# Turning kv with a TensorE transpose and a 16-column product in place of one 144-column product

## The chip, the cores and the metric

The kernel runs on one core of a Trainium2 chip. The metric is device time in microseconds (us), as the median of several executions; one more execution is recorded by the hardware profiler, and all rows below are from it.

## The reference, cut to what matters

Random-feature attention is followed by a mixture of experts with cosine routing. B = 8 batches, H = 8 heads, S = 576 positions, 64 values a head, 128 features; E = 8 experts, and x has 4608 rows of 512.

```python
phi(x) = concat([cos(x @ omega.T), sin(x @ omega.T)], -1) / sqrt(128)
q_p, k_p = phi(q), phi(k)                      # (b, h, s, 256)
kv  = einsum('bhsm,bhsd->bhmd', k_p, v)        # 256 x 64 for each head
z   = sum(k_p, axis=2)
num = einsum('bhsm,bhmd->bhsd', q_p, kv)
den = einsum('bhsm,bhm->bhs', q_p, z)          # kept away from 0
x   = (num / den), heads side by side          # (4608, 512)
logits = normed(x) @ normed(expert_emb).T / tau
e   = argmax(logits); g = softmax(logits)[e]
out = g * (relu(x @ w1[e]) @ w2[e])
```

## The kernel before

The attention runs in 32 steps, `steps[n] = (b, i)`: one batch and a pair of heads (i and i + 4) a step. The order of the work on every engine is written out by hand in the loop `for n in range(1, NS - 1)`, and what stands in it is software-pipelined: one pass of the loop holds work of steps n - 1 to n + 4. On TensorE a pass issues, in this order: `proj_q(n)` (L251), `num(n - 1)` (L373), `proj_k(n + 2)` (L238), `turns(n + 3)` (L213 and L215, TensorE transposes of k), `kv_products(n + 1)` (L324) and `kv_turn(n)` (L341 and L348).

`kv_products` leaves kv turned: the tile `kvT` holds, for each head `a` of the pair, 128 partitions (64 values for the sine half of the features, 64 for the cosine half) by 128 features. VectorE copies it out of PSUM (`kv_copy`, L334). `kv_turn(n)` then makes of it, in the PSUM region `kvnew`, what `num` needs as its moving operand: 128 features by `W` = 73 columns for each head and half. 64 of these are kv, 8 are kv times the head's part of the normed expert embedding (from which the logits are summed later on), and the last one is the sum z (from the tile `zs`, made by GpSimd in `zsum`, by the two columns of `zmask`, L348). The first 72 columns of both halves come out of one float32 product a head: `kvT[:, a]` is the stationary operand (128 x 128), and `rmat[:, i, a]`, of 2 x 72 = 144 columns, the moving one. `rmat` is block-diagonal: an identity of 64 and 8 embedding columns for each half, and zeros. ScalarE copies `kvnew` to the SBUF tile `kv` (`kv_out`, L201).

A float32 product shows as two records in the trace (two weight loads, two passes of the moving operand), a float32 transpose as one of each.

`rmat` is filled during the start-up: GpSimd clears it (L458, L459) and copies the identity into it (`set_up_unit`, L542, eight copies), VectorE adds the embedding columns (`set_up_turn`, L554). GpSimd's queue runs in order: behind `set_up_unit` come `set_up_tables`, `set_up_norms` (L506), `set_up_emb` (L514, which waits for a reciprocal on VectorE, L512, behind L509), `set_up_columns`, a weight transfer, and then the sums `zsum(0, .)` (L309 to L314) over the tile `cok`.

After the attention, 40 blocks of 128 rows go through their experts (L1054, L1087).

Of the kernel before, what the change touches and what calls it, by code (L numbers as in the profile page):

```python
# [11 lines left out]
FP32 = mybir.dt.float32  # L12
# [16 lines left out]
def kernel(  # L29
# [12 lines left out]
    nc = tc.nc  # L42
    B, H, S, Dh = q.shape
    M = omega.shape[0]
    E, D = moe_expert_emb.shape
# [3 lines left out]
    P = 128  # L49
    NPAIR = H // 2  # L50
# [13 lines left out]
    W = 64 + E + 1  # L64
# [7 lines left out]
    persist = ctx.enter_context(tc.tile_pool(name="persist", bufs=1))  # L72

    ident = persist.tile([P, P], FP32)
# [33 lines left out]

    omT2 = persist.tile([P, P], FP32)
    omT4 = persist.tile([P, 2, P], FP32)  # L110
    rmat = persist.tile([P, NPAIR, 2, 2, 64 + E], FP32)
    lsq = persist.tile([P, NSLOT, NG], FP32)
    lmax = persist.tile([P, NSLOT], FP32)
    xin_all = persist.tile([P, XBUF, XW], I32)
# [29 lines left out]
    with tc.tile_pool(name="psA", bufs=1, space=PSUM) as psA, tc.tile_pool(  # L144
# [4 lines left out]
        kvnew = ps[:, 7 * 512 + 2 * W : 7 * 512 + 6 * W].rearrange("p (h a w) -> p h a w", h=2, a=2)  # L149
# [187 lines left out]
        def kv_turn(n):  # L337
            b, i = steps[n]
            d = st[n]
            for a in range(2):  # L340
                nc.tensor.matmul(  # L341
                    kvnew[:, a, :, 0 : W - 1],
                    lhsT=d["kvT"][:, a],
                    rhs=rmat[:, i, a],
                    start=True,
                    stop=True,
                )
                nc.tensor.matmul(  # L348
                    kvnew[:, :, a, W - 1],
                    lhsT=d["zs"][:, a],  # L350
                    rhs=zmask,
                    start=True,
                    stop=True,
                )
# [110 lines left out]
        def set_up_numbers():  # L465
            for par in range(2):
                nc.gpsimd.iota(
                    tok_g[64 * par : 64 * par + 64],
                    pattern=[[2 * S, NGRP], [1, SG]], base=par * S, channel_multiplier=NCH,
                )  # L470
            nc.gpsimd.iota(tmpi[:, 0:P], pattern=[[1, P]], base=0, channel_multiplier=0)

        def set_up_tables():
            nc.gpsimd.memset(tri, 0.0)
            for e in range(1, E):
                nc.gpsimd.memset(tri[:, e, 0:e], 1.0)
            make_identity(nc, ident16)
            make_upper_triangular(nc, sltb, val=1.0, diag=False)
            nc.gpsimd.memset(onesb, 1.0)
# [53 lines left out]
                    rhs=idle.unsqueeze(1).to_broadcast([P, 2, 2 * P]), start=True, stop=True,  # L533
                )

        def set_up_unit():
            for half in range(2):
                r0 = 64 * half
                for a in range(2):
                    d0 = E if a == 0 else 0  # L540
                    for h2 in range(2):
                        nc.gpsimd.tensor_copy(  # L542
                            rmat[r0 : r0 + 64, a::2, h2, half, d0 : d0 + 64],
                            ident[r0 : r0 + 64, r0 : r0 + 64]
                            .unsqueeze(1).to_broadcast([64, NPAIR // 2, 64]),
                        )

        def set_up_turn():
            emb_t = tp_e.rearrange("p (h i e) -> p i h e", h=2, e=E)
            for half in range(2):  # L550
                r0 = 64 * half
                for a in range(2):
                    e0 = 0 if a == 0 else 64
                    nc.vector.tensor_copy(  # L554
                        rmat[r0 : r0 + 64, a::2, :, half, e0 : e0 + E], emb_t[r0 : r0 + 64, a::2]
                    )

        def part(n, which, cols):
# [25 lines left out]
        turns(0)  # L584
        copy_k(0)
        set_up_numbers()
        set_up_unit()
        set_up_tables()
        set_up_norms()
        for b in range(2):  # L590
# [52 lines left out]
        fold(1, "k")  # L643
        kv_copy(0)
        set_up_turn()
        wave(1, "co", "k")
        zsum(1, 1)
# [7 lines left out]
        kv_copy(1)  # L655
        frac(2, "k", slice(0, P))
        kv_turn(0)

        def set_up_routing(n):
# [536 lines left out]
        for n in range(1, NS - 1):  # L1196
# [43 lines left out]
            if k2:  # L1240
                frac(n + 2, "k", slice(0, P))
            kv_turn(n)
            set_up_routing(n)
            route_pe(n)
# [23 lines left out]
        hidden_products(0)  # L1268
        expert_of(1)
        kv_turn(last)  # L1270
        fold(last, "q")
        wave(last, "co", "q")
# [152 lines left out]
```

## Time and profile before

| | |
|---|---|
| median of 3 runs | 453.14 us (452.38 to 454.96) |
| profiled execution, its own time | 451.52 us |
| its span, first to last instruction | 449.7 us |
| mean granted TensorE clock | 0.994 of full speed |
| TensorE busy | 432.5 us (96%) |
| GpSimd busy | 370.0 us (82%) |
| ScalarE busy | 344.0 us (76%) |
| VectorE busy | 327.5 us (73%) |

The span leaves out what lies around the first and the last instruction, 1.8 us here. Busy time of TensorE has modelled ends, so it tells that work followed on work, and not how fast the array was fed; for that the starts of the weight loads (PEld) are read. Times within a row are from the start of the span.

### The profile page before, as it was taken

What the parts mean: (1) busy time and instruction counts of PE and PEld (TensorE: products, weight loads), DVE (VectorE), ACT (ScalarE), POOL (GpSimd) and SP (SyncE); (2) the same over time, 40 slices, a digit from 0 to 9 for tenths busy, and PEclk for the clock granted to TensorE, in tenths of its full rate; (3) what the DMA queues carried; (4) which work ended last, traced back from release to release, by engine and by line L of the source; (5) the groups of instructions that cost most, each with busy time, mean ns of one, the idle gap of its engine ahead of it and who ended that gap; (6) DMA issues with size and microseconds to landing.
All of it is one profiled execution on the core that took longest, in us unless ns stands there. A gap on an engine that the chain in (4) does not pass through costs nothing. (4 is left out here: it accounts for less than half of the span.)

```text
span 449.7 us, 18881 instructions
## 1 busy us (share of the span) xinstructions
PE 432.5 (96%) x7799; PEld 356.4 (79%) x7799; DVE 327.5 (73%) x735; ACT 344.0 (76%) x478; POOL 370.0 (82%) x507
## 2 busy tenths in 40 slices
PE   8999999999999999999999999998999999999992
PEld 4788888989888888889888888876767777777770
DVE  5679977788777789898899989999753554554450
ACT  4878988888888889888888888875556777676741
POOL 8999998988889888889899898987877778777741
PEclk9999999999999999999999999999999999999997
DMA  7999998999999989999898896559577767777530
GB/s 193 200 203 206 205 202 195 194 182 212 200 195 209 197 191 202 188 212 192 176 229 190 177 203 111 102 123 204 149 161 200 183 147 202 164 202 168 151 91 30
DMA packets 80390, 80.32 MB, mean 179 GB/s; under 512 B 32678, under 2 KB 59302, under 8 KB 80304
## 3 DMA queue, kind: packets, MB, share of 16 engines
q1 hardware_dynamic: 59616, 42.59, 40.2%
q0 software_dynamic: 19200, 35.83, 39.3%
q8 instruction: 64, 1.05, 1.0%
q10 hardware_dynamic: 1488, 0.67, 0.7%
q14 instruction: 22, 0.18, 0.1%
HBM read 72.62 MB, written 20.09 MB: 206 GB/s over the span
## 5 line engine op out<-in xcount | busy, mean ns | idle before, releaser
L1054 PEld LDWEIGHTS <-w_sb 128*128 x1280 | 74.6, 98 | 12.5 <-issue 4.3
L373 PE MATMUL ps<-kv,siq 128*64 128x73 f32 x1152 | 76.6, 229 | 0.9 <-DVE gsc L973 0.9
L1087 PE MATMUL ps<-w_sb,coq 128*128 x320 | 75.6, 379 | 0.0
L373 PE MATMUL ps<-kv,coq 128*64 128x73 f32 x1152 | 75.0, 226 | 0.1
L373 PEld LDWEIGHTS ps<-kv,siq 128*64 128x64 f32 x1152 | 58.9, 135 | 12.9 <-issue 10.8
L373 PEld LDWEIGHTS ps<-kv,coq 128*64 128x64 f32 x1152 | 60.1, 137 | 0.2 <-issue 0.2
L278 DVE SCALAR_TENSOR_TENSOR cok<-cok,ps 128x128 f32<-128x128 f32 (+1 forms) x62 | 46.3, 748 | 13.0 <-ACT cok L272 13.0
L1087 PEld LDWEIGHTS <-coq 128*128 128x128 f16 x320 | 29.6, 98 | 28.8 <-DVE coq L1069 0.6
L910 POOL DMA_INDIRECT xin_all<-rf_x,prm x40 | 42.0, 1051 | 11.9 <-issue 8.1
L309 POOL TENSOR_TENSOR zt<-sik 128x384 f32<-128x384 f32 x31 | 39.6, 1277 | 12.8 <-ACT sik L297 12.1
L278 DVE SCALAR_TENSOR_TENSOR coq<-coq,ps 128x1152 f32<-128x1152 f32 x32 | 43.2, 1351 | 5.8 <-ACT coq L272 5.6
L297 ACT ACTIVATE siq<-coq 128x1152 f32<-128x1152 f32 x32 | 37.3, 1164 | 8.3 <-DVE coq L278 7.9
L297 ACT ACTIVATE cok<-cok,pio 128x1152 f32<-128x1152 f32 x31 | 38.9, 1255 | 5.1 <-DVE cok L284 5.0
L251 PE MATMUL ps<-qr,omT 32*128 32x288 f32 x512 | 41.5, 428 | 0.9 <-DVE kvT L334 0.5
L1054 PE MATMUL ps<-qr,w_sb 128*128 128x128 f16 x640 | 39.0, 219 | 3.1 <-DMA qr<-v 2.8
L945 ACT ACTIVATE v<-xin_all 128x512 f16<-128x512 f32 x32 | 20.1, 629 | 27.8 <-issue 15.2
L238 PE MATMUL ps<-omT,kT 64*128 64x128 f32 x522 | 40.7, 284 | 0.6 <-DVE coq L278 0.6
L297 ACT ACTIVATE coq<-coq,pio 128x1152 f32<-128x1152 f32 x32 | 40.2, 1256 | 1.3 <-DVE coq L284 1.2
L314 POOL TENSOR_TENSOR zs<-zs,zt 128x128 f32<-128x128 f32 x64 | 36.2, 566 | 5.0
L1054 PE MATMUL ps<-qx,w_sb 128*128 128x128 f16 x640 | 39.0, 219 | 0.1
L272 ACT ACTIVATE cok<-ps 128x1152 f32<-128x1152 f32 x31 | 35.0, 1129 | 4.6 <-POOL zt L312 1.0
L284 DVE TENSOR_SCALAR cok<-cok 128x1152 int32<-128x1152 int32 x31 | 27.7, 892 | 14.6 <-ACT sik L297 14.1
(214 smaller groups left out, 1171.0 us busy)
## 6 DMA issues: line engine op xcount, KB each, us to landing
w_sb<-in_moe_w_dram POOLq DMA_DIRECT2D x32, 512.0 KB, 8.0
qr<-in_q_dram SPq DMA_DIRECT2D x64, 144.0 KB, 4.9
rf_x<-xb SPq DMA_DIRECT2D x30, 288.0 KB, 4.6
kr<-in_k_dram SPq DMA_DIRECT2D x58, 144.0 KB, 4.7
v<-in_v_dram SPq DMA_DIRECT2D x32, 144.0 KB, 4.6
xin_all<-in_v_dram SPq DMA_DIRECT2D x30, 144.0 KB, 4.9
w_sb<-in_k_dram SPq DMA_DIRECT2D x6, 144.0 KB, 3.1
xin_all<-rf_x,prm POOLq DMA_INDIRECT x40, 3.7
```

Source lines behind the costliest of these rows:

```text
L238: nc.tensor.matmul(kreg[:, KS[c] * P : KS[c] * P + P], lhsT=t[r0 : r0 + 64, j * P : j * P + P], rhs=omT2[r0 : r0 + 64], start=True, stop=True,
L251: nc.tensor.matmul(qreg[:, g // 2, QW * (g % 2) : QW * (g % 2) + QW], lhsT=omT4[r0 : r0 + 32, b], rhs=t[r0 : r0 + 32].rearrange("p (c b j) ...
L272: nc.scalar.activation(dst, src, AF.Copy, bias=CMAGIC, scale=1.0)
L278: nc.vector.scalar_tensor_tensor(out=dst, in0=dst, scalar=CMAGIC, in1=src, op0=ALU.subtract, op1=ALU.subtract)
L284: nc.vector.tensor_scalar(t, t, 0x7FFFFFFF, None, ALU.bitwise_and)
L297: nc.scalar.activation(st[n][which + nm], t, AF.Sin, bias=pio2 if which == "co" else 0.0, scale=-TWO_PI * SINSC,)
L309: nc.gpsimd.tensor_tensor(zt, t[:, 0:3], t[:, 3:6], ALU.add)
L314: nc.gpsimd.tensor_tensor(z, z, zt[:, 2], ALU.add)
L373: nc.tensor.matmul(nm[r0 : r0 + 64, c], lhsT=ph[:, 2 * QW * hh + 64 * c : 2 * QW * hh + 64 * c + 64], rhs=d["kv"][:, hh, half], start=(hal ...
L910: ins = nc.gpsimd.indirect_dma_start(out=t, out_offset=None, in_=x_rows[:], in_offset=bass.IndirectOffsetOnAxis(ap=prm[:, j : j + 1], axis=0),
L1054: nc.tensor.matmul(h_ps[:, f * P : f * P + P], lhsT=weights(k), rhs=d["xT"][:, c * P : c * P + P], start=(c == 0), stop=(c == 3),)
L1087: nc.tensor.matmul(y_ps, lhsT=d["hT"][:, c * P : c * P + P], rhs=weights(NW1 + c), start=(c == 0), stop=(c == NW2 - 1),)
```

## The change

`rmat` keeps only the embedding columns, 2 x 8 for each head. Each head's `kvT` is first turned by a TensorE transpose (stationary `kvT[:, a]`, moving the identity of 128 columns), which writes the 2 x 64 columns of kv, and the product with `rmat`, now of 16 columns, writes the 2 x 8 columns beside them. `set_up_unit` goes.

```diff
-    rmat = persist.tile([P, NPAIR, 2, 2, 64 + E], FP32)
+    rmat = persist.tile([P, NPAIR, 2, 2, E], FP32)
...
         def kv_turn(n):
             b, i = steps[n]
             d = st[n]
+            d0, e0 = (E, 0) if i % 2 == 0 else (0, 64)
+            for a in range(2):
+                nc.tensor.transpose(kvnew[:, a, :, d0 : d0 + 64], d["kvT"][:, a], ident)
             for a in range(2):
                 nc.tensor.matmul(
-                    kvnew[:, a, :, 0 : W - 1],
+                    kvnew[:, a, :, e0 : e0 + E],
                     lhsT=d["kvT"][:, a],
                     rhs=rmat[:, i, a],
...
-        def set_up_unit():
-            for half in range(2):
-                r0 = 64 * half
-                for a in range(2):
-                    d0 = E if a == 0 else 0
-                    for h2 in range(2):
-                        nc.gpsimd.tensor_copy(
-                            rmat[r0 : r0 + 64, a::2, h2, half, d0 : d0 + 64],
...
-                        rmat[r0 : r0 + 64, a::2, :, half, e0 : e0 + E], emb_t[r0 : r0 + 64, a::2]
+                        rmat[r0 : r0 + 64, a::2, :, half], emb_t[r0 : r0 + 64, a::2]
...
-        set_up_unit()
```

On TensorE, at the end of the first pass that holds a `kv_turn` (every later one reads alike; `128x2x72` is the output, and the names behind the arrow are the moving and the stationary operand):

```order
 L324 MATMUL ps<-cok,xin_all 64x128 x2
-L341 MATMUL ps<-rmat,kvT 128x2x72
-L348 MATMUL ps<-zmask,zs 128x2
-L341 MATMUL ps<-rmat,kvT 128x2x72
-L348 MATMUL ps<-zmask,zs 128x2
+L342 MATMUL ps<-ident,kvT 128x2x64 x2
+L344 MATMUL ps<-rmat,kvT 128x2x8
+L351 MATMUL ps<-zmask,zs 128x2
+L344 MATMUL ps<-rmat,kvT 128x2x8
+L351 MATMUL ps<-zmask,zs 128x2
 L251 MATMUL ps<-qr,omT_65 128x288 x8
```

Two transposes (now L342) stand ahead of the four products, whose order is as it was; nothing else in the queue moves.

On GpSimd, in the start-up, before:

```order
L457 MEMSET half_77 128x2
L458 MEMSET rmat 64x8x72
L459 MEMSET rmat 64x8x72
L467 IOTA w_sb 64x36 x2
L471 IOTA w_sb 128x128
L542 COPY rmat<-ident 64x2x64 x8
L474 MEMSET tri 128x64
```

and with the change:

```order
L460 MEMSET half_77 128x2
L461 MEMSET rmat 64x8x8
L462 MEMSET rmat 64x8x8
L470 IOTA w_sb 64x36 x2
L474 IOTA w_sb 128x128
L477 MEMSET tri 128x64
```

The eight copies are gone and the two clearings have a ninth of their columns; what follows keeps its order, so that it stands earlier by that much.

## Rows read from the trace of the kernel before

**Rows 1.** The page, busy time: us (share of the span), instructions.
```profile
PE 432.5 (96%) x7799; PEld 356.4 (79%) x7799; DVE 327.5 (73%) x735; ACT 344.0 (76%) x478; POOL 370.0 (82%) x507
```
**Rows 2.** Busy time by windows, steady attention: us, then each engine, granted clock, DMA.
```profile
22.00:290.00 268.00, 266.46 (x5802) 235.40 (x5804) 228.57 (x374) 231.78 (x243) 237.51 (x300) 1.00 0.91 191
```
**Rows 3.** Waits, 22 to 290 us: who waited for whom, us, times, longest.
```profile
ACT kv L201 <- PE ps L348: 17.7, 29, 0.8
...
PE ps L238 <- DVE coq L278: 0.6, 1, 0.6
PE ps L251 <- DVE kvT L334: 0.5, 1, 0.5
```
**Rows 4.** Timeline, PEld, one kv_turn and the next load: start us, us.
```profile
102.60 0.19 PEld L341 LDWEIGHTS ps<-rmat,kvT 128*128 128x128 f32 x1 [0.17 <-issue]
...
102.71 0.19 PEld L341 LDWEIGHTS ps<-rmat,kvT 128*128 128x128 f32 x1
...
102.83 0.19 PEld L348 LDWEIGHTS ps<-zmask,zs 128*128 128x128 f32 x1
...
102.95 0.19 PEld L348 LDWEIGHTS ps<-zmask,zs 128*128 128x128 f32 x1
...
103.06 0.19 PEld L341 LDWEIGHTS ps<-rmat,kvT 128*128 128x128 f32 x1
...
103.17 0.19 PEld L341 LDWEIGHTS ps<-rmat,kvT 128*128 128x128 f32 x1
...
103.30 0.19 PEld L348 LDWEIGHTS ps<-zmask,zs 128*128 128x128 f32 x1
...
103.42 0.19 PEld L348 LDWEIGHTS ps<-zmask,zs 128*128 128x128 f32 x1
...
103.63 0.20 PEld L251 LDWEIGHTS ps<-qr,omT 32*128 32x128 f32 x3
```
**Rows 5.** Timeline, PEld, transposes of k in the start-up, then a plain product.
```profile
15.54 0.11 PEld L213 LDWEIGHTS ps<-ident,w_sb 128*64 128x64 f32 x1 [0.17 <-issue]
15.57 0.14 PEld L215 LDWEIGHTS ps<-ident,w_sb 128*128 128x128 f32 x1
...
15.68 0.14 PEld L215 LDWEIGHTS ps<-ident,w_sb 128*128 128x128 f32 x1
...
15.79 0.14 PEld L215 LDWEIGHTS ps<-ident,w_sb 128*128 128x128 f32 x1
...
15.90 0.14 PEld L215 LDWEIGHTS ps<-ident,w_sb 128*128 128x128 f32 x1
...
16.01 0.10 PEld L531 LDWEIGHTS <-ident 128*128 128x128 bf16 x1
```
**Rows 6.** Tile rmat: count, ns min/median/max, first and last start us, forms.
```profile
L341 PE MATMUL ps<-rmat,kvT x128: 285/314/391, 21.9 to 293.4; 128*128 128x144 f32 x128
L542 POOL COPY rmat<-ident x8: 279/288/362, 3.2 to 4.9; 64x128 f32<-64x128 f32 x8
...
L458 POOL MEMSET rmat<- x1: 567/567/567, 1.3 to 1.3; 64x576 f32 x1
```
**Rows 7.** Timelines of the start, DVE, POOL, ACT and PE: start us, us.
```profile
8.06 0.14 DVE L509 TENSOR_SCALAR emb_n<-emb_n 8x1 f32<-8x1 f32 x1 [0.37 <-POOL emb_n L506]
...
8.47 2.03 POOL L514 TENSOR_TENSOR w_sb<-w_sb,emb_n 8x512 f32<-8x512 f32 x2 [0.44 <-DVE emb_n L512]
...
19.64 1.00 POOL L312 TENSOR_TENSOR zt<-zt,cok 128x384 f32<-128x384 f32 x1
...
20.67 1.13 ACT L272 ACTIVATE cok<-ps 128x1152 f32<-128x1152 f32 x1 [1.00 <-POOL zt L312]
...
22.97 0.41 DVE L334 COPY kvT<-ps 128x256 f32<-128x256 f32 x1
...
23.44 0.52 PE L251 MATMUL ps<-qr,omT 32*128 32x288 f32 x3 [0.49 <-DVE kvT L334]
```
**Rows 8.** Waits of PE, 285 to 450 us.
```profile
PE ps L373 <- DVE gsc L973: 0.9, 1, 0.9
```

More of the change, by code (lines that the diff above doesn't have):

```diff
@@ L534, in warm @@
                 )
-        def set_up_unit():
-            for half in range(2):
-                r0 = 64 * half
-                for a in range(2):
-                    d0 = E if a == 0 else 0
-                    for h2 in range(2):
-                        nc.gpsimd.tensor_copy(
-                            rmat[r0 : r0 + 64, a::2, h2, half, d0 : d0 + 64],
-                            ident[r0 : r0 + 64, r0 : r0 + 64]
-                            .unsqueeze(1).to_broadcast([64, NPAIR // 2, 64]),
-                        )
         def set_up_turn():
@@ L552, in set_up_turn @@
                 for a in range(2):
-                    e0 = 0 if a == 0 else 64
-                    nc.vector.tensor_copy(
-                        rmat[r0 : r0 + 64, a::2, :, half, e0 : e0 + E], emb_t[r0 : r0 + 64, a::2]
+                        nc.vector.tensor_copy(
+                        rmat[r0 : r0 + 64, a::2, :, half], emb_t[r0 : r0 + 64, a::2]
                     )
```

## The prediction

> **What bounds the kernel now.** I read the page's busy times first: TensorE is busy for 96% of the span, GpSimd for 82%, the other two for less [rows 1]. A busy TensorE is not proof of a bound, so the windows come next: from 22 to 290 us, in which nearly all of the attention's steps lie, it is busy for 266.46 of 268.00 us at a granted clock of 1.00, and no other engine for more than 237.51 [rows 2]. The waits of the same stretch say the same from the other side: TensorE itself waited 0.5 and 0.6 us for VectorE, once each, while ScalarE stood still 29 times, 17.7 us in all, until the last instruction of `kv_turn` (L348) had ended [rows 3]. So the attention goes at TensorE's pace, `kv_turn` stands in its queue and on the path of ScalarE's `kv_out` as well, and a change of its length is a change of the step. It runs 32 times; the 128 records of L341 are 2 heads x 2 passes x 32 [rows 6].
>
> Then the question is what sets the length of `kv_turn`. Its eight weight loads (128 x 128 float32, two for each of four products) start 0.11, 0.12, 0.12, 0.11, 0.11, 0.13 and 0.12 us after one another [rows 4]. What the reader is to see: behind the loads marked L348 stand products of 2 columns, behind those marked L341 products of 144, and the distances are nearly the same. Where a stream of 144 columns stands between two loads it sets 0.12 to 0.13; where one of 2 columns does, the load alone takes 0.11. From the first load to the last are 0.82 us, and 0.21 more to the first load of `proj_q`: 1.03 us.
>
> **What the columns bring.** The 144-column passes become 16-column ones, four in each `kv_turn`. They can then no longer take longer than a load, so that each such distance falls to the 0.11 of the 2-column products: the seven distances come to 7 x 0.11 = 0.77 in place of 0.82. That is 0.05 us less. No weight load goes: `kvT[:, a]` is still loaded twice for its product.
>
> **What the transposes cost.** They are two more instructions ahead of these eight, and a transpose has one load and one pass. The kernel has such transposes already: four of k follow a shorter one and precede a plain product [rows 5]. Their loads start 0.11 us apart, and the product's load starts 0.11 after the last of them, with no gap. The load of 64 columns ahead of them lets the next start after 0.03; by that a first load of 128 columns takes about 0.06 (an estimate, twice the 0.03). So in the new `kv_turn` the second transpose's load starts at 0.06, the first load of the product at 0.06 + 0.11 = 0.17, and the last load at 0.17 + 0.77 = 0.94, against 0.82. The sum is +0.12 us for each `kv_turn`.
>
> The bounds: if the first transpose's load takes the 0.11 of the float32 loads of [rows 4], the transposes cost 0.22 in all, and if the 16-column passes gain nothing, that is +0.22. With two hundredths off for the rounding of these starts in either part it is +0.09. I take +0.12, since both its prices are from rows of the same operand sizes.
>
> The Trainium skill ("TensorE: Matmul & The Clock Gate", LDWEIGHTS) gives the time of a weight load by its columns alone, P / 1.2 ns, that is 107 ns for 128 of them, whatever the product behind it streams; by that two more loads would make +0.21 us a step, and 30 steps +6.4 us. The float32 loads of the products agree with it (0.11 apart); the 64-column load of the transpose, 0.03 to the next start, is shorter than the 53 ns that it would give.
>
> **What hides it, and what does not.** The four `z` products wait for GpSimd's sums of an earlier pass and stand where they stood. Behind `kv_turn` in TensorE's queue waits `proj_q`, and on ScalarE the copy `kv_out`, then the sine of the next k; all come later by the same amount, and ScalarE was the one that waited [rows 3], so it adds nothing of its own. Of the 32, the last (at 293 us) is covered: `num` of the last step waits 0.9 us for VectorE, which is behind with work of the experts' part [rows 8]. The first is counted with the start. 30 x 0.12 = +3.6 us.
>
> **The start.** GpSimd loses eight copies of 0.288 us and most of two clearings of 0.567 [rows 6], some 3.2 us. The queue behind moves up, but only to the next thing that it waits for: L514 already waits 0.44 us for VectorE's reciprocal [rows 7], and that stands behind L509, which itself waited 0.37 for GpSimd. Without that wait L509 follows its own engine's work at 8.06 - 0.37 = 7.69, and L514 comes about 0.35 us earlier, no more. From there GpSimd's work is back to back, and so its `zt` at 19.64 ends 0.35 earlier, for which ScalarE had waited 1.00; VectorE's copy of `kvT` (22.97) follows that, and TensorE had waited 0.49 for it, at 23.44 [rows 7]. It gets back 0.35 of these, and the first `kv_turn`, longer by 0.12, still ends inside the rest of the wait: 0.49 - 0.35 = 0.14 us. I take -0.3 us. It would be nothing if VectorE's own chain is late there, and -0.49 at most, the whole wait.
>
> **The sum.** 3.6 - 0.3 = +3.3 us on the profiled execution's own time: 451.52 (its span of 449.7 and 1.8 around it) becomes 454.8. That execution lies 1.6 us below the median of the three runs shown, so against the median it is 453.14 + 3.3 = 456.4 us. With the bounds of the unknown terms: 30 x 0.09 - 0.49 = +2.2 to 30 x 0.22 = +6.6, that is 455.3 to 459.7. I give this 64 in 100.
>
> **Rivals.** *The columns decide (faster).* If loads hide behind other work and the array is fed by columns, `kv_turn` streams 2 x 2 x (144 + 2) = 584 columns before and 2 x 128 + 2 x 2 x (16 + 2) = 328 after. At 0.12 us for 144 that is 256 x 0.00083 = 0.21 us less a step, and 30 x -0.21 - 0.3 = -6.6 us: 446.5. It would decide from the point where the seven loads behind short passes come under 0.083 us apart in place of 0.11: 0.12 - 7 x 0.027 = -0.07 us a step, and 30 x -0.07 - 0.3 = -2.4. Against it stand the loads behind 2-column products, 0.11 apart, which such an array would take in no time [rows 4]. The Trainium skill ("Perfetto Trace Analysis", Transposes) asks for a transpose wherever one is logically meant, since it skips the arithmetic; it speaks for this change and gives no price, and this trace shows a transpose pass with its load at 0.11 us, as much as one of the two passes of a product. 10 in 100.
>
> *The start pays for the steps (same).* If GpSimd's 3.2 us are passed on to TensorE in full, the sum is 3.6 - 3.2 = +0.4: 453.5. The wait of L514 for VectorE speaks against it; for it, that GpSimd is busy nearly without a break in the first 22 us, and that a chain of several engines can close up elsewhere than where I look. Waits in the experts' part that take up a later start would end at the same place. 16 in 100.
>
> *The array drains between transpose and product (slower).* Where the tile of the array changes, there is a gap: 0.21 us from the last load of `kv_turn` to that of `proj_q`, against 0.11 to 0.13 inside [rows 4]. If a change from a transpose to a two-pass float32 product of the same tile costs as much, 0.1 us for the drain and 0.1 for the load that can't run ahead, the step grows by 0.32 us: 30 x 0.32 - 0.3 = +9.3, 462.4. Against it: in [rows 5] the plain product follows a transpose without a gap, though that product is bf16. 10 in 100.
>
> **How the numbers follow.** The predicted time is that of the sum, 456.4 us. The range 452.8 to 460.0 takes in the sum's own bounds and the case in which the start pays, and leaves out the two far rivals, 2 in 10. About 0.5%, 2.3 us, is what a measurement of this kernel can tell from no change. Slower by more: the sum's case but for 13 of its 64 that lie at its lower end, and the drain, 61, say 0.60; within it: the start's case and these 13, 0.30; faster: the columns, 0.10.
>
> **What would show it.** In the changed trace the loads of one `kv_turn` should be ten: two of transposes, 0.06 and 0.11 us long from start to start, then eight 0.11 apart, with 1.15 us from the first to `proj_q` in place of 1.03. TensorE should be as busy as before at the full clock, L514 should start near 8.1, and the wait ahead of the first steady `proj_q` should nearly be gone. I am wrong if the loads behind the 16-column passes lie closer than 0.11, if a gap follows the second transpose, or if the first step of the steady part comes more than 0.5 us earlier than 23.4.

## The result, and the profile after

The changed kernel takes 460.0 us in the median (459.11 to 462.08, 4 runs) against 454.05 (452.38 to 455.42) of the kernel before, measured beside it: a ratio of 1.0123 (95% interval 1.0081 to 1.0164), which is +5.6 us and between +3.7 and +7.4; the medians themselves are 5.95 apart. It is slower, as forecast, and the range of 452.8 to 460.0 just holds it; the forecast had +3.3. The profiled execution of the changed kernel lies at its median, 460.03 us with a span of 458.2. That of the kernel before, 451.52 with 449.7, lies 2.5 us below its own and under the fastest of its four runs.

One `kv_turn` of the changed kernel, as weight loads in order of time (PEld; start us, us), to be laid beside [rows 4]:

```profile
104.11 0.14 PEld L342 LDWEIGHTS ps<-ident,kvT 128*128 128x128 f32 x1 [0.17 <-issue]
104.17 0.14 PEld L342 LDWEIGHTS ps<-ident,kvT 128*128 128x128 f32 x1
104.28 0.19 PEld L344 LDWEIGHTS ps<-rmat,kvT 128*128 128x128 f32 x1
104.39 0.19 PEld L344 LDWEIGHTS ps<-rmat,kvT 128*128 128x128 f32 x1
104.50 0.19 PEld L351 LDWEIGHTS ps<-zmask,zs 128*128 128x128 f32 x1
104.61 0.19 PEld L351 LDWEIGHTS ps<-zmask,zs 128*128 128x128 f32 x1
104.72 0.19 PEld L344 LDWEIGHTS ps<-rmat,kvT 128*128 128x128 f32 x1
104.84 0.19 PEld L344 LDWEIGHTS ps<-rmat,kvT 128*128 128x128 f32 x1
104.95 0.19 PEld L351 LDWEIGHTS ps<-zmask,zs 128*128 128x128 f32 x1
105.06 0.19 PEld L351 LDWEIGHTS ps<-zmask,zs 128*128 128x128 f32 x1
...
105.27 0.20 PEld L251 LDWEIGHTS ps<-qr,omT 32*128 32x128 f32 x4
```

The reader is to see the ten loads, the first 0.06 ahead of the second, then 0.11 and 0.12 throughout, whether 128, 16 or 2 columns are streamed, and 1.16 us from the first load to `proj_q`, where it was 1.03. The steps follow at that distance; in the changed kernel, the first loads of two successive `kv_turn`s:

```profile
113.00 0.14 PEld L342 LDWEIGHTS ps<-ident,kvT 128*128 128x128 f32 x1 [0.17 <-DVE cok L278]
...
121.88 0.14 PEld L342 LDWEIGHTS ps<-ident,kvT 128*128 128x128 f32 x1 [0.17 <-DVE cok L278]
```

and in a second execution of the kernel before (the run r_before, below):

```profile
112.57 0.19 PEld L341 LDWEIGHTS ps<-rmat,kvT 128*128 128x128 f32 x1 [0.17 <-DVE cok L278]
...
121.33 0.19 PEld L341 LDWEIGHTS ps<-rmat,kvT 128*128 128x128 f32 x1 [0.17 <-DVE cok L278]
```

8.88 us a step against 8.76. The medians over all steps are 8.887 and 8.758; the difference, 0.129 us, holds in nearly every step.

The two profiled executions are 8.5 us apart, more than 31 distances of 0.129 make (4.0). The starts of the `kv_turn`s tell where the rest is. The first starts 1.8 later in the changed kernel (21.85 and 23.69 us), the fourth only 0.8 (49.91 and 50.72), since the first three steps of the kernel before are longer than its others; the run r_before below takes this up. From there to the 24th the changed kernel loses 2.3, and 20 steps of 0.129 would make 2.6. From the 24th to the 30th it takes 56.9 us in place of 53.2, which is 3.0 more than six steps explain. After the last `kv_turn`, in the experts' part, which the change doesn't touch, it is 1.3 longer. What stands in those six steps shows in the waits of TensorE, here from 28 to 283 us in the changed kernel (us, times, longest):

```profile
PE ps L342 <- issue: 1.4, 1, 1.4
PE ps L324 <- issue: 1.0, 1, 1.0
PE ps L376 <- issue: 0.6, 1, 0.6
```

"issue" is a wait for nothing that the profile shows. In the same stretch the kernel before has one wait, 0.6 us for VectorE [rows 3], and none of this kind. The longest, in the timeline of TensorE, falls between the two transposes of one `kv_turn`, of which the second waits on no semaphore of its own:

```profile
256.70 0.33 PE L342 MATMUL ps<-ident,kvT 128*128 128x128 f32 x1
258.46 0.27 PE L342 MATMUL ps<-ident,kvT 128*128 128x128 f32 x1 [1.42 <-issue]
```

The window from 255.9 to 257.2 us shows what else goes on there: one packet of the queue that the profile calls instruction (q8, 16 KB), which lands at 257.1 (queue: packets, MB, share):

```profile
q1 hardware_dynamic: 149, 0.27, 69.8%
q8 instruction: 1, 0.02, 5.2%
```

At the start, GpSimd in the changed kernel (timeline, to be laid beside [rows 7]), then VectorE's fold of `cok`:

```profile
7.27 0.58 POOL L509 TENSOR_TENSOR emb_n<-emb_n,half 8x1 f32<-8x1 f32 x1 [3.25 <-DVE w_sb L504]
8.50 2.02 POOL L517 TENSOR_TENSOR w_sb<-w_sb,emb_n 8x512 f32<-8x512 f32 x2 [0.65 <-DVE emb_n L515]
...
18.30 1.94 DVE L284 TENSOR_SCALAR cok<-cok 128x1152 int32<-128x1152 int32 x1
```

GpSimd was freed of 3.2 us and waits 3.25 for VectorE in their place. The product by 1/norm starts at 8.50, where it stood at 8.47.

### The profile page after: what moved, and what is told of

Same layout as the page of the kernel before. It is cut to its first block, busy times and chain, and to the rows that moved or that the text cites. A ratio compares the mean times of both kernels' runs of the same rounds, so it can differ in the third digit from the quotient of the medians.

```text
span 458.2 us, 19001 instructions
## 1 busy us (share of the span) xinstructions
PE 437.8 (96%) x7863; PEld 360.5 (79%) x7863; DVE 325.9 (71%) x735; ACT 341.8 (75%) x478; POOL 366.8 (80%) x499
## 5 line engine op out<-in xcount | busy, mean ns | idle before, releaser
L309 POOL TENSOR_TENSOR zt<-sik 128x384 f32<-128x384 f32 x31 | 41.7, 1344 | 17.4 <-ACT sik L297 17.0
L284 DVE TENSOR_SCALAR cok<-cok 128x1152 int32<-128x1152 int32 x31 | 29.2, 943 | 19.6 <-ACT sik L297 19.1
L309 POOL TENSOR_TENSOR zt<-cok 128x384 f32<-128x384 f32 x32 | 37.2, 1162 | 2.4
```

The lines of the kernel that those rows point to most:

```text
L284: nc.vector.tensor_scalar(t, t, 0x7FFFFFFF, None, ALU.bitwise_and)
L309: nc.gpsimd.tensor_tensor(zt, t[:, 0:3], t[:, 3:6], ALU.add)
```

## The experiments

Two theories were put to the test first. **Loads:** a `kv_turn` costs its weight loads, so that the two transposes add 0.17 us, the short passes give 0.05 back, and the rest of the difference belongs to start, execution or chip. **Columns:** the array is fed by columns, and something else made the kernel slower. Below, "stalls" are waits of TensorE for "issue", each over 0.15 us, between 28 and 283 us. Every ratio is against the kernel before as it ran beside that kernel on the same chip (medians of 455.25 to 458.6 us).

**r_after**: the changed kernel again.

> The changed kernel once more. Theory 1 (loads): a step is 8.88 us against 8.75, kv_turn 1.16 against 1.03, and the stalls of TensorE that no semaphore releases (0.8, 1.7 and 1.2 us at 233, 257 and 276 us of the first trace) stand at other places or are gone; about 4 to 6 us over the kernel before. Rival (the stalls belong to the change): they stand at the same steps again. Start: if GpSimd's freed time brings its sums beside VectorE's fold of cok each time, that fold takes 1.9 us again and the first kv_turn starts near 23.7 us; if that was one execution's, near 22.2.

1.0141 (1.0107 to 1.0176), 464.69 us against 458.01. The step is 8.887, `kv_turn` 1.16. One stall, 0.7 us at 276 us (of three in the first trace one is left, at the same product L324); the six steps from the 24th `kv_turn` take 55.98 us. The first `kv_turn` starts at 24.0 and the fold takes 1.94 us again.

**e_both**: the kernel before, with the transposes ahead of its own product.

```diff
         def kv_turn(n):
...
+            for a in range(2):
+                nc.tensor.transpose(kvnew[:, a, :, d0 : d0 + 64], d["kvT"][:, a], ident)
             for a in range(2):
                 nc.tensor.matmul(
                     kvnew[:, a, :, 0 : W - 1],
```

> The kernel before, with the two transposes issued ahead of the 144-column products, which then write the same columns again. Theory 1: the transposes cost 0.17 us a kv_turn whatever follows, so kv_turn is 1.20 us, a step 8.92, and the whole about +5 us on the kernel before. Rival (columns decide): 256 more columns, 0.21 us a step, +6.7. Rival (the 3.2 us of GpSimd matter): since GpSimd's start is that of before, the start is as before.

The step is 8.931 us: +0.173 on the kernel before, where loads gave 0.17 and columns 0.21. In its weight loads (PEld) the first product's load starts 0.17 after the first transpose's:

```profile
105.07 0.14 PEld L342 LDWEIGHTS ps<-ident,kvT 128*128 128x128 f32 x1 [0.17 <-DVE cok L278]
105.12 0.14 PEld L342 LDWEIGHTS ps<-ident,kvT 128*128 128x128 f32 x1
105.24 0.19 PEld L344 LDWEIGHTS ps<-rmat,kvT 128*128 128x128 f32 x1
```

There is no drain between a transpose and a two-pass float32 product. The whole is 1.0157 (1.0112 to 1.0202), +7.2 us, of which the steps make 5.4; it has three stalls, 2.7 us in sum.

**e_start_back**: the changed kernel, with GpSimd's work put back.

```diff
+        nc.gpsimd.memset(spare[0:64, :, :, 1], 0.0)
+        nc.gpsimd.memset(spare[64:P, :, :, 0], 0.0)
...
         set_up_numbers()
+        set_up_spare()
         set_up_tables()
```

> The changed kernel with GpSimd's two clearings and eight copies put back at their place, into a tile that nothing reads. Theory 1 (loads; the start gives next to nothing): the same time as the changed kernel within 1 us, with a step of 8.88. Rival (the freed start moves GpSimd's sums beside VectorE's fold and costs): 1 to 2 us faster than the changed kernel, with the first kv_turn at 21.9 to 22.2 us. Rival (the freed start gains): up to 3 us slower.

The first `kv_turn` starts at 23.76 us, as without that work (23.69), and the step is 8.887: in these executions the start neither gains nor costs by GpSimd's 3.2 us. The whole is 1.0095 (1.0059 to 1.0131), 2 us under the changed kernel's 1.0141, with overlapping intervals. By its time alone it would fit the rival in which the freed start costs 1 to 2 us, but that rival asked for a first `kv_turn` at 21.9 to 22.2. Its own profiled execution has more stalls than that of r_after (five, 4.0 us, against 0.7), so the 2 us don't come from a place that the trace shows.

**e_no_turn**: the changed kernel, with the transposes left out from the third step on.

```diff
-            for a in range(2):
+            for a in range(2) if n < 2 else ():
                 nc.tensor.transpose(kvnew[:, a, :, d0 : d0 + 64], d["kvT"][:, a], ident)
```

> The changed kernel with the transposes left out from the third step on, so that the 64 columns of kv are those of the first two steps; the logits' columns and z are as they should be. Theory 1: kv_turn is 1.03 - 0.05 = 0.98 us, a step 8.70, and the whole 1.5 us under the kernel before, less what the start costs. Rival (columns decide): 2 x 2 x 128 columns less, 0.43 us a step, 13 us under it.

The step is 8.714 us, `kv_turn` 0.983: 0.044 less than before, where loads gave 0.05 and columns 0.43. This is what the 16 columns bring by themselves: the loads of one `kv_turn` start 0.108 to 0.112 us apart in the median over the steps, and no closer. The loads of the products (PEld):

```profile
103.22 0.19 PEld L344 LDWEIGHTS ps<-rmat,kvT 128*128 128x128 f32 x1 [0.17 <-issue]
103.32 0.19 PEld L344 LDWEIGHTS ps<-rmat,kvT 128*128 128x128 f32 x1
103.43 0.19 PEld L351 LDWEIGHTS ps<-zmask,zs 128*128 128x128 f32 x1
```

The whole is 0.9988 (0.9957 to 1.0018), within which the expected -1.5 us lies, and no change at all as well. It has no stall.

With that the step was settled, and the stalls were open: none in the traces of the kernel before and of e_no_turn, some in all four with transposes. They could belong to the transposes, to the execution, or to the length of TensorE's code, which has 16201 records in the trace in place of 16073 (16081 in e_no_turn). The queue q8 brings 64 packets of 16 KB in every one of these traces, one for some 250 of TensorE's records, so the number of packets is not what differs.

**r_before**, **r_after_b**: both kernels again, on one chip.

> The kernel before once more, for a second trace. If the stalls of TensorE without a releaser in steps 24 to 28 are the chip's or an execution's, this kernel shows them too (2 to 4 us between the starts of the 23rd and the 29th kv_turn over the 53.2 us of its first trace). If they go with the transposes, it shows none, as in its first trace. The granted clock rises at 4.1 us in its first trace: if here too, the later rise (5.4 to 6.9 us) belongs to the changed kernel, otherwise to the execution.

> The changed kernel a third time, on the same chip as the next two: a step of 8.89 us, 4 to 7 us over the kernel before, stalls without a releaser of 1 to 4 us between 230 and 280 us.

The kernel before has no stall again (its waits of TensorE from 28 to 283 us):

```profile
PE ps L238 <- DVE coq L278: 0.8, 2, 0.5
PE ps L213 <- DMA kr<-in_k_dram: 0.2, 1, 0.2
```

Its six steps from the 24th take 53.25 us, against 53.16 in its first trace. But its first `kv_turn` starts at 24.08 us, 2.2 later than in the first trace, and its fold takes 1.94 us: the kernel before starts late too. What makes a start late shows in TensorE's first products. Two bf16 products that stand ahead of the first `proj_k` start 0.22 us after one another in the first trace and 0.43 in r_before (TensorE, first trace, then r_before):

```profile
5.46 0.59 PE L531 MATMUL ps<-ident 128*128 128x512 bf16 x2
...
6.44 0.95 PE L531 MATMUL ps<-ident 128*128 128x512 bf16 x2
```

Before 4 us such products start 0.43 apart in both. These are the two levels of the clock, 1.2 and 2.4 GHz, and the record of the granted clock agrees: it begins, at the full clock, at 4.1 us in the first trace and at 7.2 in r_before. (A window ahead of that reads 1.00 only because nothing is recorded there.) All twelve traces of this document fall in line. Where the full clock begins at 4.1 to 4.9 us (the first trace of the kernel before, e_both, e_pad2), the first `kv_turn` starts at 21.8 to 22.2 and the fold takes 0.74 or 0.75; in the other nine it begins at 5.4 to 7.2, the first `kv_turn` starts at 23.7 or later and the fold takes 1.94 or 1.95. So the late start goes with the execution's clock and not with the change. All traces in which GpSimd's work is gone are of the late kind; what that frees after an early full clock was not seen.

With equal starts (24.08 and 24.06) the fourth `kv_turn` of the two kernels starts at 51.10 us in both: the three longer steps of the changed kernel, 0.4 us, are as much as r_before loses there in two waits, for VectorE and for a transfer of k. r_after_b is 1.0167 (1.0119 to 1.0214), with four stalls of 4.5 us.

**e_pad**, **e_shift**: register additions in TensorE's queue.

```diff
+            for _ in range(4):
+                nc.tensor.reg_add(st["pad"], st["pad"], 1)
```

> The kernel before with four register additions a step in TensorE's queue, ahead of kv_turn: as many more instructions as the two transposes bring (two loads, two passes), but nothing for the array. If the stalls come from the length of the code (TensorE's instructions are fetched 16 KB at a time, and 257 us is 1.4 us after such a fetch landed late), they appear here: a step of 8.76 us, but 2 to 4 us more between the 23rd and the 29th kv_turn, +2 to +4 us in all. If the transposes themselves bring them, this kernel is the same as the kernel before within 1 us.

> The changed kernel with 64 register additions once, ahead of the first kv_turn, which moves all later code by a quarter of a fetch. If late fetches make the stalls, they change their places or go (1 to 4 us less between the 23rd and the 29th kv_turn); the start may be later by what 64 additions take, up to 3 us. If the stalls belong to the work of steps 24 to 28, they stay where they are.

Neither tested what it was made for: the additions left no instruction in the trace (16073 and 16201 records, as without them). So e_pad is a third trace of the kernel before and e_shift a fourth of the changed one. e_pad: 1.0013 (0.9986 to 1.004), no stall, step 8.758. Its profiled execution took 56.4 us for the six steps, though, with waits for VectorE and for a transfer of k, 2.7 us of them in these steps: the kernel before can lose time there too, by waits that have a releaser. e_shift: 1.0181 (1.0124 to 1.0238), four stalls, 3.1 us.

In e_shift a stall costs more than its own length. Behind the one that ends at 123.2 us the granted clock falls to half, 1.2 GHz, from 125.6 to 129.0 us, while TensorE is busy (windows: us, then each engine, granted clock, DMA):

```profile
123.20:125.60 2.40, 2.39 (x32) 2.06 (x31) 1.31 (x3) 0.76 (x2) 1.62 (x3) 1.00 1.06 254
125.60:129.00 3.40, 3.40 (x54) 2.83 (x48) 2.11 (x2) 2.96 (x3) 2.46 (x2) 0.50 0.89 156
```

The two steps there take 10.19 and 10.48 us, 2.9 over their length, and the stall is 0.9 of that. The same follows the stalls that end at 281.0 us here, at 280.4 in r_after_b and at 206.6 in e_shift2 (below). The traces without stalls have no such stretch in the attention, and behind most stalls there is none either.

**e_pad2**: the kernel before, with two bf16 products of one column a step.

```diff
+            for a in range(2):
+                nc.tensor.matmul(
+                    kvnew[:, a, 0, 0:1], lhsT=one[:, 0:P], rhs=one[:, 0:1], start=True, stop=True
+                )
```

> The four register additions of the earlier run left no instruction in the trace (16073 on TensorE, as before), so here the kernel before gets two bf16 products of one column a step instead, ahead of kv_turn, into a column that the 144-column product overwrites: four more records a step, as with the transposes (16201 in all), at some 0.05 us each on the array. A step should be 8.84 to 8.88 us. If the stalls without a releaser between 230 and 283 us come from the length of TensorE's code, they appear here, 1 to 4 us, and the whole is 4 to 7 us over the kernel before; if the float32 transposes bring them, none appear and the whole is 2.5 to 4 us over it.

The step is 8.806, cheaper than expected (the two add 0.048, so that the 31 steps make +1.5). Stalls appear without the transposes of the change, two, small (waits of TensorE, 28 to 283 us):

```profile
PE ps L238 <- DVE coq L278: 1.2, 1, 1.2
PE ps L324 <- issue: 0.4, 1, 0.4
PE ps L378 <- issue: 0.2, 1, 0.2
```

The whole is 1.0067 (1.0025 to 1.0109), +3.1 us: 1.5 from the steps and 1.6, with an interval of some 2 either way, which the steps don't explain.

**e_shift2**: the changed kernel, with 32 such products once, at the start.

```diff
+            for _ in range(32 if n == 0 else 0):
+                nc.tensor.matmul(
+                    kvnew[:, 0, 0, 0:1], lhsT=one[:, 0:P], rhs=one[:, 0:1], start=True, stop=True
+                )
```

> The changed kernel with 32 bf16 products of one column once, ahead of the first kv_turn: 64 more instructions, so that all later code lies a quarter of a 16 KB fetch further on. If the stalls come from where the fetches fall in the steps, they move or change in sum by over 1 us between the 23rd and the 29th kv_turn; if not, they stay at the products L324 and L376 of steps 24 to 28, 2 to 5 us in sum. The first kv_turn is up to 2 us longer.

Three of the six stalls are elsewhere, at 58, 164 and 207 us, and three are in steps 24 to 28 as before (0.2, 0.2 and 0.8 us). The six steps lost 1.1 us beyond their own length (55.06) in place of 3.0, and the 20 steps ahead of them, which no stall had touched in the first two traces of the changed kernel, took 183.1 us in place of 178.0. The work of all these steps is as it was, so no step's work by itself is what stalls. Waits of TensorE, 28 to 283 us:

```profile
PE ps L324 <- issue: 0.9, 2, 0.8
PE ps L381 <- issue: 0.9, 2, 0.7
PE ps L347 <- issue: 0.9, 1, 0.9
PE ps L238 <- issue: 0.9, 1, 0.9
```

The whole is 1.0215 (1.0159 to 1.0271).

All 28 stalls of the eight traces that have any share one thing: each ends 1.15 to 2.20 us after a packet of q8 has landed, 25 of them within 1.15 to 1.60. The packets come some 6 us apart, so that by chance one stall in six would. "Issue" waits are found in the experts' part of eight of the twelve traces as well, with and without the change (r_before has nine, 3.6 us; the first trace of the kernel before none). Those follow no packet at a fixed distance and are another matter.

## Why the prediction was right, and what it lacked

*What bounds the kernel.* Right: 0.13 us more in `kv_turn` is 0.129 more in every step, and ScalarE's wait for `kv_turn` only grew. No other engine gave anything back.

*What the columns bring.* -0.05 us forecast; -0.044 in the step of e_no_turn. The distance between loads does not fall under 0.108 with 16 columns, which refutes the rival in which the columns decide: it needed 0.083.

*What the transposes cost.* +0.17 forecast; +0.173 in e_both. The estimate of 0.06 for a transpose's load of 128 columns, from the 0.03 of one of 64, is in the trace (104.11 to 104.17). The sum of +0.12 a step measured 0.129, 31 times and not 30: 4.0 us in place of 3.6. The Trainium skill ("TensorE: Matmul & The Clock Gate", LDWEIGHTS) gives the time of a weight load by its columns alone; by an estimate from that, 107 ns for 128 columns, the two loads would make +0.21 a step. The traces decide otherwise: 0.06 after the first transpose's load, 0.11 after the second's, as between the transposes of [rows 5], and 0.11 after a product's.

*The drain* between transpose and product does not exist: 0.11 us from the last transpose's load to that of the 16-column product, 0.12 in e_both to that of the 144-column one.

*The start.* -0.3 us forecast, nothing found: with GpSimd's work put back the start is the same. The step that failed is that L514 would move up by 0.35, to near 8.1 us. As L517 of the changed kernel it starts at 8.50, since the freed GpSimd waits 3.25 us for VectorE one product earlier. The prediction read one execution, with the full clock from 4.1 us and VectorE early; in r_before, with the full clock from 7.2, GpSimd already waited 0.63 for VectorE ahead of L506. So the rival in which the start pays is refuted for starts of this late kind, and the -0.3 for an early one stays untested.

*What the sum lacked.* Stalls of TensorE without a releaser: 0.7 to 4.5 us in the seven traces with the transposes, at other places in part each time, and in three of these traces stretches at half the clock behind them. Steps of 4.0 us leave 1.6 of the measured +5.6 (+3.7 to +7.4). The changed kernel measured +6.5 in r_after, +7.7 in r_after_b and +8.3 in e_shift, where 2.5 to 4.3 are left; stalls and clock are of that size, but each trace is of one execution. Shown: stalls come without these transposes (e_pad2 has two, though only 0.6 us), not by the work of one step (e_shift2 moves them), and each follows a packet of instructions. That they are waits for code is argued from this and not shown, and so is the length of the code as their cause: none is in the four traces with the shorter code, but e_pad, made to test that, did not lengthen it. Why some packets come too late is open.

The experts' part is open as well. From the last `kv_turn` to the end the kernel before took 157.0 us in its first trace and 162.7 in r_before, and the changed one 158.3 to 165.1.

*What was luck.* The direction and the price of a step were reasoned, and they held. That the range held the time was luck: its upper end was made for transposes at 0.22 us a step, and what filled it were stalls, for which the prediction has no term. (Its lower bound of 0.09 takes three hundredths off 0.12, where two in either part make 0.08; nothing hangs on it.)

## What to carry to other kernels

Where products of few columns follow one another on TensorE, count weight loads and not columns: taking 128 columns off a 144-column float32 product gave 0.011 us a pass, and one more 128 x 128 float32 load with its pass cost 0.06 to 0.11. The type counts too: a bf16 load of that size, with a pass of one column, cost 0.024 (e_pad2). A work item that is freed on another engine is worth what the next thing in its queue waits for; look for that wait in more than one execution before counting on it, and where two traces of one kernel start differently, look first at when the clock rose in each. And an engine that is busy without a break also reads its code: more instructions in its queue may cost more than their time on the array, which is argued here and not shown.

## What the runs showed that was not expected

The instruction supply of TensorE as a likely cost: at 16201 records in place of 16073, waits of up to 2.0 us each between instructions that nothing else holds up (r_after_b, L324), each behind a packet of q8, and at four of them a granted clock of 0.50 soon after.

A fold of `cok` on VectorE that takes 0.74 us in the first trace of the kernel before, at 17.63, takes 1.94 in r_before, at 18.69, where it lies beside GpSimd's sums (L309 and L312). Both are the same kernel; the later execution had its first TensorE products slower (the transpose L578 took 0.42 us for 0.27), its full clock beginning at 7.2 us in place of 4.1, and came 1.1 us later to that place. The 2.2 us by which its first `kv_turn` is later shrink to 1.2 by the fourth.
